# Linear-attention and feed-forward block on one core: half of the queries put with tokens on partitions, their denominators formed on VectorE

## The chip, the core and the metric

One core of one Trainium2 chip runs the whole kernel. The metric is the device time of one execution in microseconds. The kernel before took 170.02 us, the median of three runs (169.81, 170.02, 170.82).

## What is computed

The input x has 2048 tokens of 512 numbers, in bfloat16. The reference, cut to what matters:

```python
def attention(x, wqkv, wo):              # 32 heads of 16 columns
    q, k, v = split(x @ wqkv)
    phi = lambda t: jnp.where(t > 0, t + 1, jnp.exp(t)) + 1e-6
    pq, pk = phi(q), phi(k)
    kv  = einsum("bhsd,bhse->bhde", pk, v)
    z   = einsum("bhsd->bhd", pk)
    num = einsum("bhqd,bhde->bhqe", pq, kv)
    den = einsum("bhqd,bhd->bhq", pq, z)[..., None] + 1e-6
    return (num / den).reshape(B, S, D) @ wo

h  = x + attention(layernorm(x), wqkv, wo)
h2 = h + relu(layernorm(h) @ w1) @ w2    # w1 is 512 x 1792, w2 is 1792 x 512
```

There is no softmax: one 16x16 matrix kv and one vector z per head serve all tokens. The quotient num / den needs one denominator per token and head.

## The kernel before, in words

**Tiles.** The 2048 tokens are 16 tiles of 128 (t = 0 to 15) and four blocks of 512 (c = 0 to 3, four tiles each). Layer-normed tiles exist with tokens on partitions (ln_nat, which shares h_nat's memory) and transposed (lnT, columns on partitions). PSUM is one tile bk of eight banks of 128x512 float32.

**Order.** Nothing schedules the kernel: it is under a manual schedule, and a string ORDER names every operation as a word, op.index.index. A loop at the end (from L561 on) calls the functions op_... in that order. Each engine runs its own words in the order of the string, and semaphores hold back what depends on another engine. In the words of the matrix operations the last number before a slice is the PSUM bank, so the string also says which bank is reused when. All DMAs are issued by SP's queue (SyncE), in the order of the string: loads, transposes through the DMA, and the output.

**Stage 1, keys.** Per tile: bn_stats and bn_aggr (S, A, L237, L238), the reciprocal deviation on ScalarE as Ln and Exp (R, L243, L244), the normalisation (N, L262), the transpose to lnT (T on TensorE with E on ScalarE for tiles 0 to 3, X, a DMA transpose, L302, for the others), four matmuls with wk (K, L310), then phi in four instructions: Exp and Relu on ScalarE (F, U, L328, L331), min and add on VectorE (M, D, L335, L338). G (L362) accumulates layer-normed x times phi(k) over all tiles in banks 4 to 7. z (L381) sums phi(k) over the tokens.

**Stage 2, queries.** Q (L318) makes a 128x512 tile of q with *columns* on partitions and a block's 512 tokens in the free dimension; qF, qU, qM, qD (or qW, L343, which reads PSUM and does relu and add at once) turn it into phi(q), pqT. kv (L403), m (L415) and mA (L418, ScalarE, two instructions) fold kv and wo into one matrix m_sb. For a block's denominators TensorE multiplies pqT with z spread over heads (dn, L459: 16 matmuls with a free size of 8); ScalarE takes Ln (dnl, L465) and Exp of its negative, repeated 16 times per head (dnx, L472, two instructions of two tiles); the reciprocals are transposed tile by tile into rd (dt, a DMA transpose, L491; rt on TensorE with re or rv for two tiles); dm (L495, VectorE) multiplies pqT with rd into pqs, two column groups at a time. h (L505) multiplies pqs with m_sb, four matmuls per token tile, hD (L511) adds x.

**Stage 3, feed-forward.** Per tile: statistics (s, a, L239, L240), mean removed (n, L269), transpose into lnT again (x, L303, DMA). p (L521) is one of 14 column groups of the first product for a block, pA (ScalarE, L527) or pD (VectorE, L532) its relu, two groups at a time. f (L541) is the second product of a token tile, 14 matmuls in two halves of seven; fo (L549, VectorE) scales and adds h, fd (L556) stores. The products of one block lie between the attention of the next ones.

Of the kernel before, what the change touches and what calls it, by code (L numbers as in the profile page):

```python
# [9 lines left out]
ALU = mybir.AluOpType  # L10
# [20 lines left out]
Q.1.3.1 qF.1.2.2 m.0.4 m.1.5 rv.2 Q.3.1.7 qW.1.0.2 m.3.6 Q.2.3.2 dt.3 qM.1.2.2 mA.0.2 qW.1.2.2 dt.0 dt.1 m.2.5
Q.2.1.4 dn.1.0 mA.2.2 dm.0.0.2 Q.2.2.1 dm.0.2.2 dnl.1 dnx.1.2.2 h.3.6 dnx.1.0.2 h.1.5 rt.6.3 hD.3 qF.2.2.2 dt.7
s.3 re.6 h.0.0 dt.4 qU.2.2.2 hD.1 dt.5 a.3 hD.0 s.1 s.0 a.1 qM.2.2.2 a.0 Q.3.0.6 Q.2.0.3 n.3 h.2.5 n.0 dm.1.0.2
Q.3.3.1 x.3 dm.1.2.2 qF.3.0.2 hD.2 n.1 s.2 Q.3.2.0 qU.2.0.2 qF.2.0.2 h.5.2 h.6.3 a.2 qU.3.0.2 qM.2.0.2 h.4.7 n.2
qF.3.2.2 x.0 qD.2.0.2 t.2.5 qD.2.2.2 hD.4 x.1 hD.6 h.7.4 dn.2.6 hD.5 hD.7 e.2 dnl.2 qM.3.0.2 p.0.0.5 dnx.2.2.2
p.0.13.7 p.0.1.6 p.0.8.2 p.0.9.3 dnx.2.0.2 qD.3.0.2 s.4 l2.7.3 p.0.11.4 pA.0.0.2 dt.11 l2.0.3 dt.9 dt.10 r.0.4
qM.3.2.2 qW.3.2.2 s.6 dt.8 p.0.12.6 s.7 pD.0.12.2 p.0.3.1 p.0.2.0 pA.0.8.2 dn.3.2 p.0.5.7 dnl.3 p.0.4.6 a.7
dm.2.0.2 pA.0.2.2 dnx.3.0.2 dnx.3.2.2 dm.2.2.2 pD.0.4.2 h.9.0 h.8.5 p.0.6.6 p.0.7.7 dt.13 dt.12 s.5 dt.14
# [10 lines left out]
p.2.13.7 f.11.3.0.7 p.3.12.4 pD.2.12.2 f.9.6.0.7 f.9.6.7.7 f.10.7.0.7 pA.3.12.2 pA.3.0.2 f.11.3.7.7 f.10.7.7.7
f.8.2.0.7 f.12.1.0.7 f.8.2.7.7 f.14.5.0.7 f.13.4.0.7 f.15.0.0.14.3.1 f.14.5.7.7 fo.11 fo.9 fo.10 fd.10 fd.11  # L50
fo.15.3.1 fo.8 f.12.1.7.7 fd.9 f.13.4.7.7 fd.8 f.15.0.0.14.0.2 fo.14 fo.12 fd.12 fo.13 fd.15.3.1 fo.15.0.2
f.15.5.0.14.2.1 fd.13 fd.14 fd.15.0.2 fo.15.2.1 fd.15.2.1
# [4 lines left out]
def kernel(  # L57
# [10 lines left out]
    nc = tc.nc  # L68
# [41 lines left out]
    ones = const.tile([P, 1], BF16, name="ones")  # L110
# [3 lines left out]
    erep = const.tile([P, P], BF16, name="erep")  # L114
# [9 lines left out]
    z_sb = big.tile([P, KD], F32, name="z_sb")  # L124
    acts = [big.tile([P, KF, CW], BF16, name=f"at{i}") for i in range(2)]
# [15 lines left out]
    r4 = rd  # L141
# [19 lines left out]
    unit = {"k": 0, "q": NT}  # L161
# [24 lines left out]
    def op_masks():  # L186
        nc.gpsimd.memset(mask[:], 1.0)
        keep(mask3, mask3, [[-DH, P // DH], [0, DH]], 0, 1)
        keep(mask3, mask3, [[DH, P // DH], [0, DH]], DH - 1, -1)
        nc.gpsimd.memset(mask_h[:], 1.0)  # L190
        keep(mask_h[:], mask_h[:], [[0, KD], [-DH, Q4]], 0, 1)
        keep(mask_h[:], mask_h[:], [[0, KD], [DH, Q4]], DH - 1, -1)
        nc.gpsimd.memset(erep[:], 1.0)
        for q in range(KD):
            rows = erep[q * Q4 : (q + 1) * Q4, :]
            keep(rows, rows, [[1, P]], 0, -DH)
            keep(rows, rows, [[-1, P]], DH - 1, DH)
# [154 lines left out]
    op_W = lambda t, n: relu_add_of("k", t, n)  # L352
    op_qF = lambda c, j, n: exp_of("q", c * KD + j, n)
# [70 lines left out]
    def op_d4(c, b):  # L424
        at_bank["d4", c] = b
        for jb in range(KD):
            nc.tensor.matmul(
                bk[jb * Q4 : (jb + 1) * Q4, b, :], lhsT=zhd[:, jb, :], rhs=pqT[c][:, jb, :],
                start=True, stop=True,
            )  # L430

    def op_dl4(c):
        nc.scalar.activation(
            out=ld[:, c % 2, :], in_=bk[:, at_bank["d4", c], :], func=ACT.Ln, bias=eps6[:], scale=1.0
        )
# [156 lines left out]
```

## Time and profile before

| what | value |
|---|---|
| time, median of three runs | 170.02 us |
| span of the profiled execution, first to last instruction | 168.8 us |
| TensorE matmul busy | 163.1 us, 97% |
| VectorE busy | 104.4 us, 62% |
| ScalarE busy | 65.1 us, 39% |
| GpSimd busy | 4.8 us, 3% |
| share of the span on the chain that ended last, by engine | PE 85%, DVE 7%, DMA 4% |
| DMA, mean over the span | 92 GB/s |

The times listed are those of the three runs; the profiled execution is known by its span, and the median stands 1.2 us above it. PE is TensorE's matmuls, PEld its weight loads, DVE VectorE, ACT ScalarE, SPq the queue of SyncE that issues the DMAs. A matmul's duration in a row holds the depth of the array too, and consecutive matmuls overlap, so what one costs in a stream is the distance between starts: a row of the chain "76.29 3.02 PE bk L541 x14" is 14 matmuls with 512 columns in 3.02 us, 0.216 us each.

### The profile page before, as it was taken

How to read it: one execution, taken by the hardware profiler on the slowest of the kernel's cores; microseconds unless marked ns; L12 is line 12 of the kernel's file. 1: busy time of each engine (PE TensorE's matmuls, PEld its weight loads, DVE VectorE, ACT ScalarE, POOL GpSimd, SP SyncE). 2: the span in 40 equal slices, each digit the busy share in tenths (PEclk: the TensorE clock that was granted, in tenths of full speed). 3: DMA queues.
4: the chain of work that ended last, by engine and by line, in shares of the span. 5: the costliest groups of instructions: out<-in, count | busy, mean ns of one | idle time of the engine just before them, and what ended most of it. 6: DMA issues, size and time to landing. Idle time of an engine off the chain costs nothing.

```text
span 168.8 us, 2286 instructions
## 1 busy us (share of the span) xinstructions
PE 163.1 (97%) x855; PEld 78.0 (46%) x871; DVE 104.4 (62%) x205; ACT 65.1 (39%) x97; POOL 4.8 (3%) x21
## 2 busy tenths in 40 slices
PE   7989999999999999999999999999999999999993
PEld 5344344445644454444444444444444444444553
DVE  3899998997668999699819879215102432050251
ACT  3698775875879947432000003004320420400000
POOL 7400000000000000000000000000000000000000
PEclk9999999999999999999999999999999999999999
DMA  4975575689533353534130015500320000002023
GB/s 112 352 245 97 97 66 124 176 270 378 174 64 65 77 138 87 134 62 95 37 62 0 31 31 122 126 4 0 62 93 0 31 0 4 0 0 93 0 65 94
DMA packets 30491, 15.49 MB, mean 92 GB/s; under 512 B 23184, under 2 KB 29328, under 8 KB 30480
## 3 DMA queue, kind: packets, MB, share of 16 engines
q1 hardware_dynamic: 30480, 15.34, 35.5%
q8 instruction: 7, 0.11, 0.3%
q14 instruction: 4, 0.03, 0.1%
HBM read 7.86 MB, written 2.10 MB: 59 GB/s over the span
## 4 chain that ended last, share of the span: by engine, by line
PE 85%; DVE 7%; DMA 4%; issue 1%; SPq 0%
PE bk L541 29%; PE bk L521 28%; PE bk L505 8%; PE bk L318 8%; PE bk L362 6%; PE bk L310 4%; DVE st L237 3%; DMA x_nat<-in_A_x_dram 2%; DMA lnT<-h_nat 2%; DVE h_nat L262 2%; PE bk L459 1%; DVE eb L335 1%; PE bk L403 1%; PE bk L415 1%; SPq L201 0%
## 5 line engine op out<-in xcount | busy, mean ns | idle before, releaser
L541 PE MATMUL bk<-w_sb,at 128*128 128x512 bf16 (+2 forms) x247 | 50.1, 355 | 0.3
L521 PE MATMUL bk<-lnT,w_sb 128*128 128x512 bf16 x219 | 50.0, 379 | 0.3
L527 ACT ACTIVATE at<-bk 128x1024 bf16<-128x1024 f32 x14 | 14.2, 1023 | 57.4 <-PE bk L521 57.4
L541 PEld LDWEIGHTS <-at 128*128 128x128 bf16 x252 | 23.6, 98 | 25.4 <-ACT at L527 0.3
L549 DVE SCALAR_TENSOR_TENSOR gT<-bk,rstd,h_nat 128x512 bf16<-128x512 f32 (+2 forms) x18 | 12.2, 689 | 35.7 <-PE bk L541 35.6
L521 PEld LDWEIGHTS <-w_sb 128*128 128x128 bf16 x224 | 21.8, 98 | 25.8
L532 DVE TENSOR_SCALAR at<-bk 128x1024 bf16<-128x1024 f32 x14 | 17.1, 1218 | 12.8 <-PE bk L521 12.6
L328 ACT ACTIVATE eb<-bk 128x1024 bf16<-128x1024 f32 (+1 forms) x18 | 16.6, 928 | 6.6 <-PE bk L310 4.8
L310 PE MATMUL bk<-wk_sb,lnT 128*128 128x512 bf16 x63 | 15.3, 380 | 0.4 <-ACT lnT L291 0.3
L505 PE MATMUL bk<-m_sb,pqs 128*128 128x512 bf16 x63 | 15.4, 380 | 0.1
L318 PE MATMUL bk<-lnT,wq_sb 128*128 128x512 bf16 x61 | 15.1, 379 | 0.1
L362 PE MATMUL bk<-at,h_nat 128*128 128x512 bf16 x55 | 13.5, 379 | 0.1
L331 ACT ACTIVATE rb<-bk 128x1024 bf16<-128x1024 f32 (+1 forms) x14 | 12.5, 904 | 0.3 <-PE bk L310 0.3
L511 DVE TENSOR_TENSOR h_nat<-bk,x_nat 128x512 bf16<-128x512 f32 x16 | 10.5, 680 | 2.9 <-PE bk L505 2.9
L237 DVE BATCH_NORM_STATS2 st<-x_nat 128x6 f32<-128x512 bf16 x16 | 10.8, 680 | 2.4 <-DMA x_nat<-in_A_x_dram 2.4
L239 DVE BATCH_NORM_STATS2 st<-h_nat 128x6 f32<-128x512 bf16 x16 | 10.7, 683 | 0.1
L310 PEld LDWEIGHTS <-lnT 128*128 128x128 bf16 x64 | 6.0, 98 | 8.4 <-ACT lnT L291 1.0
L362 PEld LDWEIGHTS <-h_nat 128*128 128x128 bf16 x64 | 6.2, 98 | 7.4 <-issue 0.2
L505 PEld LDWEIGHTS <-pqs 128*128 128x128 bf16 x64 | 5.9, 98 | 7.9 <-DVE pqs L495 1.8
L318 PEld LDWEIGHTS <-wq_sb 128*128 128x128 bf16 x64 | 5.9, 98 | 6.4
L472 ACT ACTIVATE wk_sb<-ld 128x1024 bf16<-128x1024 f32 x8 | 8.1, 1050 | 0.1
L335 DVE TENSOR_SCALAR eb<-eb 128x1024 bf16<-128x1024 bf16 (+1 forms) x18 | 6.8, 383 | 0.9 <-ACT eb L328 0.9
(63 smaller groups left out, 93.5 us busy)
## 6 DMA issues: line engine op xcount, KB each, us to landing
out_dram<-gT SPq DMA_DIRECT2D x15, 128.0 KB, 1.9
w_sb<-in_B_w_dram SPq DMA_DIRECT2D x2, 896.0 KB, 9.8
x_nat<-in_A_x_dram SPq DMA_DIRECT2D x2, 512.0 KB, 6.3
w_sb<-in_B_w_dram SPq DMA_DIRECT2D x2, 512.0 KB, 9.5
x_nat<-in_A_x_dram SPq DMA_DIRECT2D x3, 256.0 KB, 4.6
w_sb<-in_B_w_dram SPq DMA_DIRECT2D x2, 384.0 KB, 3.5
wk_sb<-in_A_wqkv_dram SPq DMA_DIRECT2D x2, 256.0 KB, 4.3
wq_sb<-in_A_wqkv_dram SPq DMA_DIRECT2D x2, 256.0 KB, 4.9
```

What stands on the lines that cost most here:

```text
L237: op_S = lambda t: nc.vector.bn_stats(out=st[:, t, :], in_=x_nat[:, t, :])
L310: nc.tensor.matmul(bk[:, b, :], lhsT=lnT[c][:, kd, j * P : (j + 1) * P], rhs=wk_sb[:, kd, :], start=(kd == 0), stop=(kd == KD - 1),)
L318: nc.tensor.matmul(bk[:, b, :], lhsT=wq_sb[:, kd, j * P : (j + 1) * P], rhs=lnT[c][:, kd, :], start=(kd == 0), stop=(kd == KD - 1),)
L328: nc.scalar.activation(out=buf(eb, kind, i, n), in_=bank(at_bank[kind, i], n), func=ACT.Exp)
L331: nc.scalar.activation(out=buf(rb, kind, i, n), in_=bank(at_bank[kind, i], n), func=ACT.Relu)
L362: nc.tensor.matmul(bk[:, KD + kd, :], lhsT=ln_nat[:, t, kd * P : (kd + 1) * P], rhs=pk(t)[:, 0, :], start=(t == 0), stop=(t == NT - 1),)
L505: nc.tensor.matmul(bk[:, b, :], lhsT=pqs[:, (c * KD + jb) % NQ, j * P : (j + 1) * P], rhs=m_sb[:, jb, :], start=(jb == 0), stop=(jb == KD ...
L521: nc.tensor.matmul(bk[:, b, cols], lhsT=w1_sb[:, kd, f * P : (f + 1) * P], rhs=lnT[c][:, kd, cols], start=(kd == 0), stop=(kd == KD - 1),)
L527: nc.scalar.activation(out=acts[c % 2][:, f : f + n, :], in_=bank(at_bank["p", c, f], n), func=ACT.Relu)
L532: nc.vector.tensor_scalar(out=acts[c % 2][:, f : f + n, :], in0=bank(at_bank["p", c, f], n), scalar1=0.0, scalar2=None, op0=ALU.max,)
L541: nc.tensor.matmul(bk[:, b, 0 : w * P], lhsT=acts[c % 2][:, f, j * P : (j + 1) * P], rhs=w2_sb[:, f, k * P : (k + w) * P], start=(f == 0), ...
L549: nc.vector.scalar_tensor_tensor(out=o_t[:, t % NO, cols], in0=bk[:, at_bank["f", t, k], 0 : w * P], scalar=rstd2[:, t : t + 1], in1=h_nat ...
```

## The change

Blocks 0 and 1 keep their way. For blocks 2 and 3 (tiles 8 to 15):

- Y takes Q's place: four matmuls per *token tile* with lnT as the stationary side and wq as the moving one, so that phi(q) comes out with tokens on partitions. The words yF, yU, yM, yD do what qF, qU, qM, qD do, two tiles at a time; the words qW are gone.
- The denominators are not made by TensorE any more (dn.2, dn.3, with their dnl, dnx, dt and dm, are gone). z is first spread over 128 identical rows: zd (VectorE) makes four diagonal matrices, zr (TensorE) multiplies them with ones, four matmuls with 128 columns, and zC (ScalarE) copies the result to zrep. Then per two tiles: dT (VectorE) multiplies phi(q) with zrep into float32 products, dR (VectorE) sums each 16 of them, dl and dx (ScalarE) take Ln and the repeated Exp, dy (VectorE) multiplies phi(q) in place.
- The quotient is then transposed tile by tile to pqs by a DMA transpose (ty). h and all that follows stay.
- Of the relus of the first product, pA has 12 instead of 14 instructions and pD 16 instead of 14. re now does both copies of rd from PSUM (rv is gone), and qU and qD take the place of two qW of block 1.
- The whole ORDER is written anew. The first two Y stand between the last Q and h of block 0. The attention of blocks 2 and 3 now lies between the second products of block 0 and those of block 1. Loads of wv, wq, wo and w2 are put in among the first transposes.
- The constant erep, which nothing read, is gone; ones grows to 128x128.

```diff
-Q.1.3.1 qF.1.2.2 m.0.4 m.1.5 rv.2 Q.3.1.7 qW.1.0.2 m.3.6 Q.2.3.2 dt.3 qM.1.2.2 mA.0.2 qW.1.2.2 dt.0 dt.1 m.2.5
+dnx.0.0.2 dnx.0.2.2 l1.2.2 l1.0.2 dt.1 dt.3 dt.0 qF.1.0.2 qU.1.0.2 rt.2.7 Q.1.3.6 Y.14.4 kx m.1.1 m.0.0 qF.1.2.2
...
+    def op_Y(t, b):
+        c, j = divmod(t, CT)
+        at_bank["y", t] = b
+        for kd in range(KD):
+            nc.tensor.matmul(
+                bk[:, b, :], lhsT=lnT[c][:, kd, j * P : (j + 1) * P], rhs=wq_sb[:, kd, :],
+                start=(kd == 0), stop=(kd == KD - 1),
+            )
...
+    def op_zd():
+        nc.vector.tensor_tensor(
+            out=zdg[:], in0=ident.rearrange("p (o n) -> p o n", o=1).broadcast_to([P, KD, P]), in1=z_on(P),
+            op=ALU.mult,
+        )
+
+    def op_zr(b):
+        at_bank["zr"] = b
         for jb in range(KD):
             nc.tensor.matmul(
...
+                bk[:, b, jb * P : (jb + 1) * P], lhsT=ones[:], rhs=zdg[:, jb, :], start=True, stop=True
+            )
+
+    def op_zC():
+        nc.scalar.activation(out=zrep[:], in_=bank(at_bank["zr"]), func=ACT.Copy)
+
+    def toks(t, n):
+        return pqT[t // CT][:, t % CT : t % CT + n, :]
+
+    def op_dT(t, n):
+        nc.vector.tensor_tensor(
+            out=prod[:, 0:n, :], in0=toks(t, n), in1=zrep.broadcast_to([P, n, D]), op=ALU.mult
+        )
+
+    def op_dR(t, n):
+        nc.vector.tensor_reduce(
+            out=den[:, t * H : (t + n) * H], in_=prod[:, 0:n, :].rearrange("p t (h r) -> p (t h) r", r=DH),
+            axis=mybir.AxisListType.X, op=ALU.add,
+        )
+
+    def op_dl(t, n):
+        cols = den[:, t * H : (t + n) * H]
+        nc.scalar.activation(out=cols, in_=cols, func=ACT.Ln, bias=eps6[:], scale=1.0)
+
+    def op_dx(t, n):
+        src = den[:, t * H : (t + n) * H].rearrange("p (h o) -> p h o", o=1)
...
+            out=rn[:, t % CT : t % CT + n, :].rearrange("p t (h r) -> p (t h) r", r=DH),
+            in_=src.broadcast_to([P, n * H, DH]), func=ACT.Exp, scale=-1.0,
+        )
+
+    def op_dy(t, n):
+        nc.vector.tensor_tensor(out=toks(t, n), in0=toks(t, n), in1=rn[:, t % CT : t % CT + n, :], op=ALU.mult)
+
+    def pqs_of(t):
+        c, j = divmod(t, CT)
+        i = c * KD % NQ
+        return pqs[:, i : i + KD, j * P : (j + 1) * P]
+
+    def op_ty(t):
+        nc.sync.dma_start_transpose(out=pqs_of(t), in_=toks(t, 1)[:, 0, :])
```

**ScalarE, from the reciprocals of block 0 to the folded matrix.** Before, L465 is dnl, L472 dnx, L328 qF, L418 mA:

```order
L465 ACTIVATE ld<-bk,eps_74 128x128
L472 ACTIVATE wk_sb<-ld 128x1024
L328 ACTIVATE eb<-bk 128x1024
L472 ACTIVATE wk_sb<-ld 128x1024
L328 ACTIVATE eb<-bk 128x1024
L418 ACTIVATE m_sb<-bk 128x1024 x2
L465 ACTIVATE ld<-bk,eps_74 128x128
```

Now, with the line numbers of the changed kernel (L504 dnl, L511 dnx, L334 qF, L337 qU, L522 re, L429 mA):

```order
L504 ACTIVATE ld<-bk,eps_74 128x128
L511 ACTIVATE wk_sb<-ld 128x1024 x2
L334 ACTIVATE eb<-bk 128x1024
L337 ACTIVATE rb<-bk 128x1024
L334 ACTIVATE eb<-bk 128x1024
L337 ACTIVATE rb<-bk 128x1024
L522 ACTIVATE rd<-bk 128x4x128
L429 ACTIVATE m_sb<-bk 128x1024 x2
L504 ACTIVATE ld<-bk,eps_74 128x128
```

The two dnx stand together, and two qU and one re have come between them and the two mA; before, relu and add of block 1 were VectorE's (L343), and so was the copy into rd.

**VectorE, in the first product of block 0.** Before, L338 and L343 end the phi of the last queries, L239 is s, L532 pD, L495 dm of block 2, L511 hD:

```order
L335 TENSOR_SCALAR eb<-eb 128x1024
L343 SCALAR_TENSOR_TENSOR pqT_88<-bk,eb 128x1024
L239 BN_STATS st_101<-h_nat 128x6 x2
L532 TENSOR_SCALAR at_94<-bk 128x1024
L240 BN_AGGR mv_102<-st_101 128x2
L495 TENSOR_TENSOR pqs<-pqT_87,rd 128x1024 x2
L532 TENSOR_SCALAR at_94<-bk 128x1024
L239 BN_STATS st_101<-h_nat 128x6
L511 TENSOR_TENSOR h_nat<-bk,x_nat 128x512
L239 BN_STATS st_101<-h_nat 128x6
```

Now (L344 yD, L550 hD, L236 s, L455 dT, L571 pD, L266 n, L460 dR):

```order
L344 TENSOR_TENSOR pqT_86<-rb,eb 128x1024
L236 BN_STATS st_104<-h_nat 128x6
L455 TENSOR_TENSOR prod<-pqT_86,zrep 128x1024
L571 TENSOR_SCALAR at_97<-bk 128x1024 x2
L266 TENSOR_SCALAR hn<-h_nat,mv_105 128x512
L237 BN_AGGR mv_105<-st_104 128x2
L266 TENSOR_SCALAR hn<-h_nat,mv_105 128x512
L236 BN_STATS st_104<-h_nat 128x6
L571 TENSOR_SCALAR at_97<-bk 128x1024
L237 BN_AGGR mv_105<-st_104 128x2
L266 TENSOR_SCALAR hn<-h_nat,mv_105 128x512
L460 TENSOR_REDUCE den<-prod 128x64
```

The multiplication by z and the reductions stand in the same queue as the relus of the first product and the means that the transposes of block 1 wait for.

**SyncE's queue, in the first 25 us.** Before, L201 and L204 are loads, L302 the transposes of stage 1:

```order
L201 DMA x_nat<-in_A_x_dram 128x2048 x2
L204 DMA wq_sb<-in_A_wqkv_dram 128x2x512
L302 DMA_TRANSPOSE lnT_82<-h_nat 128x4x128 x4
L302 DMA_TRANSPOSE lnT_83<-h_nat 128x4x128 x2
L302 DMA_TRANSPOSE lnT_84<-h_nat 128x4x128 x2
L302 DMA_TRANSPOSE lnT_83<-h_nat 128x4x128 x2
L204 DMA wq_sb<-in_A_wqkv_dram 128x2x512
L302 DMA_TRANSPOSE lnT_84<-h_nat 128x4x128 x2
```

Now (L198, L201 loads, L299 transposes):

```order
L201 DMA wv_sb<-in_A_wqkv_dram 128x2x512
L198 DMA x_nat<-in_A_x_dram 128x2048
L201 DMA w_sb<-in_B_w_dram 128x3x512
L299 DMA_TRANSPOSE lnT_81<-h_nat 128x4x128 x2
L201 DMA wq_sb<-in_A_wqkv_dram 128x2x512
L299 DMA_TRANSPOSE lnT_81<-h_nat 128x4x128 x2
L201 DMA w_sb<-in_B_w_dram 128x4x512
L299 DMA_TRANSPOSE lnT_82<-h_nat 128x4x128
L201 DMA wq_sb<-in_A_wqkv_dram 128x2x512
L299 DMA_TRANSPOSE lnT_82<-h_nat 128x4x128
L299 DMA_TRANSPOSE lnT_83<-h_nat 128x4x128 x2
L201 DMA wo_sb<-in_A_wo_dram 128x2x512
```

Loads of wv, wq, w2 and wo now stand ahead of and between the transposes, where before a single load of wq stood ahead of ten transposes.

More of the change, by code (lines that the diff above doesn't have):

```diff
@@ L34 @@
[L34 to L38, printed above, removed]
@@ L49 @@
[L49 to L52, printed above, removed]
+table lx.0.1 lx.1.1 lx.2.2 lk.0.2 masks lx.4.2 const S.0 lk.2.2 lx.6.2 A.0 warmf.4.3 S.1 lx.8.4 R.0.1 lv.2.2 A.1
@@ L109 @@
     eps6 = const.tile([P, 1], F32, name="eps6")
-    ones = const.tile([P, 1], BF16, name="ones")
+    ones = const.tile([P, P], BF16, name="ones")
     ident = const.tile([P, P], BF16, name="ident")
@@ L192, in op_masks @@
         keep(mask_h[:], mask_h[:], [[0, KD], [DH, Q4]], DH - 1, -1)
[L193 to L197, printed above, removed]
     def op_lx(t, n):
@@ L381, in op_z @@
             nc.tensor.matmul(
-                bk[:, b, jb : jb + 1], lhsT=part[:, jb * P : (jb + 1) * P], rhs=ones[:],
+                bk[:, b, jb : jb + 1], lhsT=part[:, jb * P : (jb + 1) * P], rhs=ones[:, 0:1],
                 start=(i == 0), stop=(i == len(parts) - 1),
@@ L440, in op_rp @@
-    def op_rp(c, jb, b):
-        at_bank["rp", c, jb] = b
-        rows = slice(jb * Q4, (jb + 1) * Q4)
-        nc.tensor.matmul(
-            bk[:, b, :], lhsT=erep[rows, :], rhs=r4[rows, c, :], start=True, stop=True
-        )
-    def op_rm(c, jb, n):
-        i = (c * KD + jb) % NQ
-        nc.vector.tensor_tensor(
-            out=pqs[:, i : i + n, :], in0=bank(at_bank["rp", c, jb], n), in1=pqT[c][:, jb : jb + n, :],
-            op=ALU.mult,
-        )
+            out=rn[:, t % CT : t % CT + n, :].rearrange("p t (h r) -> p (t h) r", r=DH),
@@ L454, in op_dn, with op_rE @@
+    def op_rE(t):
+        nc.scalar.activation(out=pqs_of(t), in_=at_bank["ry", t], func=ACT.Copy)
     def op_dn(c, b):
```

79 lines of the change are left out of this document (44 added, 35 removed).

## The prediction

> **What bounds the kernel now.** I read the page first, then the chain of work that ended last, then the timeline around each wait of the chain, and the groups by line and shape for durations.
>
> ```profile
> PE 163.1 (97%) x855; PEld 78.0 (46%) x871; DVE 104.4 (62%) x205; ACT 65.1 (39%) x97; POOL 4.8 (3%) x21
> ...
> PEclk9999999999999999999999999999999999999999
> DMA  4975575689533353534130015500320000002023
> ```
>
> TensorE is busy 97% of the span at full granted clock. The chain says the same in order of time (start, length, what):
>
> ```profile
> 41.53 0.38 PE bk L459 x16
> ...
> 42.79 0.89 PE bk L403 x16
> ...
> 50.35 1.97 PE bk L505 x8
> ...
> 61.40 0.38 PE bk L459 x16
> ...
> 69.57 0.38 PE bk L459 x16
> ...
> 71.70 2.00 PE bk L505 x8
> ...
> 76.29 3.02 PE bk L541 x14
> ...
> 166.18 0.35 DVE gT L549
> ```
>
> From 21.1 to 166.2 us every piece of the chain is TensorE, but for slivers of 0.05 called issue. 14 matmuls of 512 columns take 3.02 us, so 0.216 each: that is the price of TensorE's work here, and there is little beside it. The two pieces of eight L505 show what waiting is left: eight cost 1.73, and they took 1.97 and 2.00, so 0.24 and 0.27 us were lost to pqs that came late. One more wait is in the start:
>
> ```profile
> 10.85 14.66 SPq L302 DMA_TRANSPOSE lnT<-h_nat  x10
> ...
> 19.94 1.03 PE L362 MATMUL bk<-at,h_nat 128*128 128x512 bf16 x4
> ...
> 21.09 0.55 PEld L310 LDWEIGHTS <-lnT 128*128 128x128 bf16 x4 [0.63 <-DMA lnT<-h_nat]
> 21.10 1.04 PE L310 MATMUL bk<-wk_sb,lnT 128*128 128x512 bf16 x4
> ```
>
> Four matmuls from 19.94 would end their slots at 20.80; the next begins at 21.10, when a transpose has landed: 0.30 lost. So from about 10 us on the whole kernel gives away some 0.8 us, and the change can win only by taking work from TensorE or by these 0.8. It can lose wherever the new order makes TensorE wait.
>
> **TensorE's work.** Y has as many matmuls of 512 columns as the Q it replaces: 32 for 32, nothing. dn.2 and dn.3 go: the pieces at 61.40 and 69.57, 0.76 us. zr is four matmuls of 128 columns; 16 of that width (L403) took 0.89, so 0.056 each and 0.22 together. The counts of transposes, of warming matmuls and of halves of f are the same. Net **-0.54 us**, and it counts in full since nothing but TensorE is on the chain there.
>
> **The folded matrix comes later.** ScalarE between the denominators of block 0 and m_sb:
>
> ```profile
> 28.27 1.02 ACT L331 ACTIVATE rb<-bk 128x1024 bf16<-128x1024 f32 x1
> ...
> 29.18 1.03 ACT L328 ACTIVATE eb<-bk 128x1024 bf16<-128x1024 f32 x1
> ...
> 30.08 1.04 ACT L331 ACTIVATE rb<-bk 128x1024 bf16<-128x1024 f32 x1
> ...
> 41.37 0.54 PE L459 MATMUL bk<-zhd,pqT 128*128 128x8 bf16 x16
> ...
> 41.95 0.37 ACT L465 ACTIVATE ld<-bk,eps 128x128 f32<-128x128 f32 x1
> ...
> 49.91 2.00 ACT L472 ACTIVATE wk_sb<-ld 128x1024 bf16<-128x1024 f32 x2
> ...
> 52.72 0.59 ACT L483 ACTIVATE rd<-bk 128x512 bf16<-128x512 bf16 x1
> ```
>
> Back to back, an Exp or Relu of 128x1024 starts 0.91 after the one before it (28.27, 29.18, 30.08). dnl starts at 41.95; nothing ahead of it on ScalarE or TensorE is changed in amount, so I keep that. Then, start to start: dnl 0.40, two dnx 1.94, four qF and qU 3.64, re 0.55, first mA 0.91, and the second mA takes 1.02 to its end: 41.95 + 8.46 = 50.4. The new qU are what makes it late; qW on VectorE kept ScalarE free. TensorE, from dn.0 at 41.37: dn 0.38, kv 0.89, two Q 1.73, rt 0.22, Q 0.86, three Y 2.59, four m 0.86, dn.1 0.38, zr 0.22, sum 8.13: h begins at 49.5. Its first two matmuls need only the first half of m_sb and pqs; the third, due at 49.93, waits for 50.4. **+0.5 us.** pqs is ready by then: the first dnx ends at 43.4, three DMA transposes at most 1.47 us apart (ten in 14.66, above) and 2.5 from the last issue to its landing give 48.8, and two dm of 0.69 make 50.2.
>
> ```profile
> rd<-wk_sb SPq DMA_TRANSPOSE x14, 2.5
> lnT<-h_nat SPq DMA_TRANSPOSE x12, 2.5
> ```
>
> Block 1 follows from there: dnl, dnx, yF, yU, dnx end near 54.5, the last dt lands at 57.1, the second dm ends near 58.5, and h.5, due at 58.0, needs it in its third matmul: **+0.1**. Some 0.1 more lies in kv and dn.1, which meet their inputs to within 0.1. Against these stand the two losses of before at pqs, **-0.51**, for the words that met them there are gone or are the ones just counted. Sum of this stage: +0.2 of waits over before.
>
> **VectorE's new denominators.** What they cost is in no row; the nearest:
>
> ```profile
> L532 DVE TENSOR_SCALAR at<-bk 128x1024 bf16<-128x1024 f32 x14 | 17.1, 1218 | 12.8 <-PE bk L521 12.6 <-remote 0.2
> ...
> L549 DVE SCALAR_TENSOR_TENSOR gT<-bk,rstd,h_nat 128x512 bf16<-128x512 f32 x15 | 11.1, 748 | 27.0 <-PE bk L541 26.9
> ...
> L239 DVE BATCH_NORM_STATS2 st<-h_nat 128x6 f32<-128x512 bf16 x16 | 10.7, 683 | 0.1
> L511 DVE TENSOR_TENSOR h_nat<-bk,x_nat 128x512 bf16<-128x512 f32 x16 | 10.5, 680 | 2.9 <-PE bk L505 2.9
> ...
> L369 DVE TENSOR_TENSOR at<-at,at 128x1024 f32<-128x1024 f32 x5 | 6.1, 1223 | 0.1
> ...
> L335 DVE TENSOR_SCALAR eb<-eb 128x1024 bf16<-128x1024 bf16 x14 | 5.7, 414 | 0.9 <-ACT eb L328 0.9
> L269 DVE TENSOR_SCALAR hn<-h_nat,mv 128x512 bf16<-128x512 bf16 x16 | 5.3, 342 | 0.1
> L495 DVE TENSOR_TENSOR pqs<-pqT,rd 128x1024 bf16<-128x1024 bf16 x8 | 5.2, 687 | 2.8 <-DMA rd<-wk_sb 2.6 <-issue 0.2
> ...
> L240 DVE BATCH_NORM_AGGREGATE mv<-st 128x2 f32<-128x6 f32 x16 | 2.6, 170 | 0.1
> ```
>
> dT reads two bf16 and writes float32: between 0.69 (L495, all bf16) and 1.22 (L369, all float32); I take 1.22, as it writes what L369 writes. dR reads 1024 float32 and writes 64: at least 0.41 (L335, the cheapest pass over 1024), at most 2.4 (twice L369, if a pass costs each of its short sums something); 1.22 again, and L239, a reducing pass over 512 in 0.68, points there. The Trainium skill (VectorE: DVE Perf Modes, "The perf-mode tier table") says that tensor_reduce has only the slowest mode, one element per cycle whatever the type, and its cycle table would make that 1.13 us for 1024 elements, an estimate of that page; with it the sum below would be shorter by 0.3 us.
>
> ```profile
> 60.99 2.48 DVE L511 TENSOR_TENSOR h_nat<-bk,x_nat 128x512 bf16<-128x512 f32 x4
> ```
>
> ```profile
> 60.00:80.00 20.00, 19.89 (x121) 9.31 (x123) 17.89 (x31) 9.60 (x13) 0.00 (x0) 1.00 0.46 106
> 80.00:100.00 20.00, 19.89 (x92) 9.11 (x93) 14.42 (x32) 0.50 (x2) 0.00 (x0) 1.00 0.13 27
> ```
>
> In these windows (PE, PEld, DVE, ACT, POOL busy) VectorE had 2.1 and 5.6 us free and ScalarE 10.4 and 19.5, so there is room, but the queue is in order. From the first dm of block 1 (57.1) to the second dy, which releases ty for h.15, VectorE has 2 dm, 4 hD, 5 s with 5 a and 5 n, 4 yM, 4 yD, 4 dT, 3 dR, 4 pD, 2 fo, 2 dy: 44 instructions, 29.6 us by row means (yD as dm), some 27 if each starts 0.06 before the end of the last, as four L511 in 2.48 instead of 2.72 do. With 2.5 for the transpose pqs is there between 86.6 and 89.3. TensorE from h.5 (58.0) to h.15 has 4 h, t, 14 p, 7 halves of f, 3 p, 2 h: 30.7 us, 88.7. Slack between -0.6 and 2.1, middle 0.8. I put **0** in the sum and keep +0.6 for the range. dl, dx and zC are covered by ScalarE's free time; were that gone, an ACT pair would cost 1.4 per two tiles. The banks of the first product (pD behind dT) come free with 0.5 to spare by the same addition.
>
> **The start.** 1664 KB of loads (384 + 512 of w2, two of 256 of wq, 256 of wo) now lie ahead of or between the first ten transposes, where 256 KB lay.
>
> ```profile
> w_sb<-in_B_w_dram SPq DMA_DIRECT2D x2, 384.0 KB, 3.5
> ```
>
> ```profile
> 17.65 3.40 DMA lnT<-h_nat
> ```
>
> ```profile
> PEld L310 <- DMA lnT<-h_nat: 1.0, 2, 0.6
> ```
>
> One transpose took 3.40 from issue to landing, and that made the 0.30 of before, the longer of two waits. Now the transposes of tiles 8 and 9 each follow a load (512 and 256 KB) directly, and the matmuls that read them stand at nearly the same places of TensorE's order as before. Two transposes at 3.4 instead of 2.5 give up to +1.8; if all fits, -0.3 is regained. The nearest row is the old wait: I take **+0.2**. The end is as before: the same last half rows, then fo and one store.
>
> **Sum.** -0.54 + 0.2 + 0 + 0.2 = -0.14: a span of 168.8 - 0.1 = 168.7 us, and with the 1.2 us by which the median stands above the span, **169.9 us**. Its own range, from the bounds above (start -0.3 to +1.8, VectorE 0 to +0.6, waits ±0.3): 168.9 to 171.3.
>
> **Rivals.** *The new order closes the gaps.* Then -0.54, -0.8 of old waits and none new, at most 0.3 more from the start: 168.4. For it: each wait that I found is 0.5 or less, within the error of such additions. Against: m_sb's 0.5 comes from ten instructions in a queue whose distances are measured.
>
> *The reductions bound the feed-forward stage (slower).* dR of tiles 10, 8 and 14 stand ahead of the dy that h.15 needs. With a slack of 0.8 it decides from 1.5 us per dR on; at the bound of 2.4 it costs 3 x 1.18 - 0.8 = 2.7: 172.6. For it: 64 short sums per instruction have no row here. Against: L239 and L369. The same page of the Trainium skill, "Rules for kernel authors", calls tensor_reduce the slowest VectorE operation and advises against it on a hot path; no run shows it yet.
>
> *Loads delay the first transposes (slower).* From 10 to 25 us the DMA row shows five to seven tenths with transposes almost alone. 1664 KB more at the page's best 378 GB/s are 4.5 us of 15, three tenths. It decides from a landing time of about 3 us on, and at 3.4 or more for the transposes of tiles 9 and 13 it costs 1.3 beside the +0.2: 171.2.
>
> ```profile
> GB/s 112 352 245 97 97 66 124 176 270 378 174 64 65 77 138 87 134 62 95 37 62 0 31 31 122 126 4 0 62 93 0 31 0 4 0 0 93 0 65 94
> ```
>
> **How the numbers follow.** A measurement of this kernel can tell about 1%, 1.7 us, from no change. Chances: the forecast 0.58, closed gaps 0.14, reductions 0.11, loads 0.17. Faster by over 1% means under 168.3: more than half of the closed gaps' 0.14 and a little of the forecast, 0.10. Slower by over 1%, above 171.7: most of the reductions' 0.11 and a third of the loads' 0.17, 0.14. Within 1%: 0.76. The range reaches down to the closed gaps and up past the loads: 168.4 to 171.6.
>
> **What would show it.** Right: L459 with 32 matmuls and 1.1 us busy; a wait of near 0.5 us before the third matmul of the first h, ended by m_sb on ScalarE; TENSOR_REDUCE near 1.2 us; waits on TensorE from 60 us on below 0.5 in all. Wrong: TENSOR_REDUCE above 1.5 with TensorE waiting for pqs or for a bank that pD frees; PEld waits on DMA lnT<-h_nat above 1.3 us (now 1.0); or a span under 167.5, which my waits at m_sb do not allow.

## The result, and the profile after

The changed kernel took 172.13 us (median of four runs, 171.58 to 172.34); the kernel before, on the same chip, 170.38 us (169.81 to 170.82). The ratio is 1.0106, 95% interval 1.007 to 1.0142: 1.75 us slower, where 169.9 us was forecast. The profiled execution took 171.92 us with a span of 170.2.

The page after, busy time of each engine, the granted clock and the DMA engines' share in 40 slices:

```profile
PE 163.8 (96%) x843; PEld 77.2 (45%) x843; DVE 115.7 (68%) x215; ACT 66.9 (39%) x102; POOL 2.3 (1%) x12
...
PE   7999969999999999999999999999999999999993
...
PEclk9999999999999999999999999999999999999999
DMA  4997899993040530014313350055400000000322
```

TensorE still has the end, at full clock. Its first slice under 9 after the warming is the sixth, 21.3 to 25.5 us, and there the DMA engines are full where they had been five to seven tenths. Windows of the span after (length, then busy time of PE, PEld, DVE, ACT, POOL, then clock, DMA share, GB/s) put the loss into one of them:

```profile
20.00:40.00 20.00, 18.31 (x85) 7.97 (x84) 17.63 (x32) 11.37 (x16) 0.00 (x0) 1.00 1.07 249
60.00:80.00 20.00, 20.00 (x97) 9.12 (x96) 19.89 (x36) 8.25 (x12) 0.00 (x0) 1.00 0.17 34
80.00:100.00 20.00, 20.00 (x95) 9.09 (x93) 17.61 (x25) 4.98 (x7) 0.00 (x0) 1.00 0.34 67
100.00:160.00 60.00, 60.00 (x287) 27.85 (x286) 25.83 (x41) 9.47 (x14) 0.00 (x0) 1.00 0.16 38
```

From 60 us on TensorE never waits, though VectorE is busy 19.89 of 20 us where its new denominators begin. All that was lost, was lost early. The waits after (engine, line, releaser, total, times, longest):

```profile
PEld L307 <- DMA lnT<-h_nat: 3.7, 5, 1.7
```

This row stood at 1.0 before, and 1.3 was the mark that the prediction set for being wrong. L307 is K, the keys; L299 is X, its DMA transpose. The timeline of SyncE's queue, and below it TensorE's:

```profile
17.59 1.19 SPq L299 DMA_TRANSPOSE lnT<-h_nat  x1
18.83 0.58 SPq L201 DMA_DIRECT2D wq_sb<-in_A_wqkv_dram  x1
19.51 3.81 SPq L299 DMA_TRANSPOSE lnT<-h_nat  x3
```

```profile
19.34 1.89 PE L373 MATMUL bk<-at,h_nat 128*128 128x512 bf16 x8
21.70 1.04 PE L307 MATMUL bk<-wk_sb,lnT 128*128 128x512 bf16 x4 [0.46 <-DMA lnT<-h_nat]
23.96 1.04 PE L307 MATMUL bk<-wk_sb,lnT 128*128 128x512 bf16 x4 [1.23 <-DMA lnT<-h_nat]
```

Eight matmuls from 19.34 fill their slots until 21.07, at 0.216 each; the keys of tile 8 begin at 21.70: 0.63 lost. Those four end their slots at 22.56, and the keys of tile 9 begin at 23.96: 1.40 lost. Together 2.0 us, where the same place lost 0.30 before. The transpose of tile 8, issued at 17.59 behind a load of 512 KB, landed just ahead of 21.70, 4.1 us later; that of tile 9, issued behind the load at 18.83, is the longest piece of the chain there:

```profile
19.51 4.41 DMA lnT<-h_nat
```

### The profile page after: what moved, and what is told of

Same layout as the page of the kernel before. It is cut to its first block, busy times and chain, and to the rows that moved or that the text cites. A ratio compares the mean times of both kernels' runs of the same rounds, so it can differ in the third digit from the quotient of the medians.

```text
span 170.2 us, 2241 instructions
## 1 busy us (share of the span) xinstructions
PE 163.8 (96%) x843; PEld 77.2 (45%) x843; DVE 115.7 (68%) x215; ACT 66.9 (39%) x102; POOL 2.3 (1%) x12
## 4 chain that ended last, share of the span: by engine, by line
PE 79%; DVE 7%; ACT 6%; DMA 4%; issue 1%
PE bk L580 28%; PE bk L560 28%; PE bk L544 8%; PE bk L373 5%; PE bk L307 4%; DVE st L234 3%; DMA lnT<-h_nat 3%; PE bk L315 3%; PE bk L324 3%; DMA x_nat<-in_A_x_dram 2%; ACT eb L334 2%; ACT rb L337 2%; DVE h_nat L259 1%; ACT m_sb L429 1%; DVE at L344 1%
## 5 line engine op out<-in xcount | busy, mean ns | idle before, releaser
L560 PE MATMUL bk<-lnT,w_sb 128*128 128x512 bf16 x224 | 50.0, 379 | 0.0
L560 PEld LDWEIGHTS <-w_sb 128*128 128x128 bf16 x224 | 21.9, 98 | 26.2
L566 ACT ACTIVATE at<-bk 128x1024 bf16<-128x1024 f32 x12 | 12.3, 1021 | 52.5 <-PE bk L560 52.5
L588 DVE SCALAR_TENSOR_TENSOR gT<-bk,rstd,h_nat 128x512 bf16<-128x512 f32 (+2 forms) x18 | 12.1, 688 | 24.6 <-PE bk L580 20.3
L571 DVE TENSOR_SCALAR at<-bk 128x1024 bf16<-128x1024 f32 x16 | 19.2, 1219 | 13.5 <-PE bk L560 13.5
L334 ACT ACTIVATE eb<-bk 128x1024 bf16<-128x1024 f32 (+1 forms) x18 | 16.5, 928 | 5.5 <-PE bk L307 5.5
L307 PE MATMUL bk<-wk_sb,lnT 128*128 128x512 bf16 x64 | 15.7, 380 | 1.9 <-DMA lnT<-h_nat 1.7
L337 ACT ACTIVATE rb<-bk 128x1024 bf16<-128x1024 f32 (+1 forms) x17 | 15.7, 924 | 3.2 <-PE bk L315 3.1
L544 PE MATMUL bk<-m_sb,pqs 128*128 128x512 bf16 x64 | 15.3, 379 | 0.1
L550 DVE TENSOR_TENSOR h_nat<-bk,x_nat 128x512 bf16<-128x512 f32 x16 | 10.8, 679 | 1.8 <-PE bk L544 1.8
L236 DVE BATCH_NORM_STATS2 st<-h_nat 128x6 f32<-128x512 bf16 x16 | 10.9, 688 | 0.2
L307 PEld LDWEIGHTS <-lnT 128*128 128x128 bf16 x64 | 5.8, 98 | 10.0 <-DMA lnT<-h_nat 3.7
L544 PEld LDWEIGHTS <-pqs 128*128 128x128 bf16 x64 | 6.1, 98 | 7.4 <-DVE pqs L534 0.5
L240 ACT ACTIVATE rstd<-mv,eps 128x2 f32<-128x2 f32 (+2 forms) x14 | 4.2, 299 | 10.3 <-DVE mv L237 5.3
L315 PE MATMUL bk<-lnT,wq_sb 128*128 128x512 bf16 x32 | 8.0, 379 | 0.0
L324 PE MATMUL bk<-wq_sb,lnT 128*128 128x512 bf16 x32 | 7.6, 379 | 0.0
```

Of the source, the lines that this page charges most:

```text
L307: nc.tensor.matmul(bk[:, b, :], lhsT=lnT[c][:, kd, j * P : (j + 1) * P], rhs=wk_sb[:, kd, :], start=(kd == 0), stop=(kd == KD - 1),)
L315: nc.tensor.matmul(bk[:, b, :], lhsT=wq_sb[:, kd, j * P : (j + 1) * P], rhs=lnT[c][:, kd, :], start=(kd == 0), stop=(kd == KD - 1),)
L324: nc.tensor.matmul(bk[:, b, :], lhsT=lnT[c][:, kd, j * P : (j + 1) * P], rhs=wq_sb[:, kd, :], start=(kd == 0), stop=(kd == KD - 1),)
L334: nc.scalar.activation(out=buf(eb, kind, i, n), in_=bank(at_bank[kind, i], n), func=ACT.Exp)
L337: nc.scalar.activation(out=buf(rb, kind, i, n), in_=bank(at_bank[kind, i], n), func=ACT.Relu)
L544: nc.tensor.matmul(bk[:, b, :], lhsT=pqs[:, (c * KD + jb) % NQ, j * P : (j + 1) * P], rhs=m_sb[:, jb, :], start=(jb == 0), stop=(jb == KD ...
```

## The experiments

The theory after the result: the loads put among the first transposes delay them, and nothing else of the change costs anything. The rivals: the new order of keys and evictions makes the waits by itself; VectorE's denominators or the later folded matrix cost, and the start hides it. All ratios are to the kernel before on the same chip; medians of before were 169.9 to 170.0 us there.

### Loads moved off the transposes (a_loads_back), and only five of them (d_few)

```diff
 a_loads_back, in ORDER of the change:
-lv.2.2 l2.0.3 lq.2.2 l2.10.4 lq.0.2 lo.2.2 l2.3.4 lv.0.2 l2.7.3 lo.0.2 (among X.4 to X.15), l1.2.2 l1.0.2
+lq.0.2 behind lx.12.4; lq.2.2 behind X.13; lv, lo and l1 behind X.14; l2 behind x.3
 d_few, in ORDER of the change:
-lv.2.2 l2.0.3 l2.10.4 lq.0.2 lo.2.2 (ahead of and between X.4 to X.10)
+lq.0.2 behind lx.12.4; l2.10.4 lo.2.2 lv.2.2 l2.0.3 behind X.14
```

> The changed kernel with its loads moved off the first transposes, nothing else: one half of wq ahead of the ten transposes (256 KB, as in the kernel before), the other after the eighth, wv, wo and w1 after the twelfth, w2 after the first transposes of stage 3. Theory (loads in the same queue delay the transposes of tiles 8 and 9, and TensorE loses 2.0 us there): both transposes land about 2.5 us after issue, TensorE's waits at L307 fall from 2.0 to 0.3 us or less, span 168.2 to 168.5, ratio to the kernel before 0.995 to 0.999. Rival (VectorE's new order issues the two transposes too late, loads or not): the wait stays above 1 us, span above 169.5, ratio 1.005 or more.

> The change with only the loads that stand ahead of the transposes of tiles 8 and 9 moved out of their way (one load of queries' weights and the later loads stay among the transposes). If only loads right ahead of a transpose that TensorE waits for count, this is as good as all loads moved back: 1.003 to 1.006. If every load among the transposes costs its share: 1.007 to 1.010.

Measured: a_loads_back 170.54 us, ratio 1.0041 (1.0025 to 1.0056), between the two expectations; d_few 170.50 us, 1.0042 (1.0027 to 1.0058), as the first of its two said. So the loads account for 0.65 of 1.06%, 1.1 us, and five of the twelve, those right ahead of the transposes of tiles 8 and 9 among them, for all of that. Some 0.8 us must have another cause. The waits, the timeline of TensorE and one piece of the chain of a_loads_back show where it lies:

```profile
PEld L306 <- DMA lnT<-h_nat: 2.9, 4, 1.1
```

```profile
20.26 1.03 PE L306 MATMUL bk<-wk_sb,lnT 128*128 128x512 bf16 x4
21.86 1.04 PE L306 MATMUL bk<-wk_sb,lnT 128*128 128x512 bf16 x4 [0.56 <-DMA lnT<-h_nat]
...
23.59 1.03 PE L306 MATMUL bk<-wk_sb,lnT 128*128 128x512 bf16 x4
25.27 1.04 PE L306 MATMUL bk<-wk_sb,lnT 128*128 128x512 bf16 x4 [0.65 <-DMA lnT<-h_nat]
```

```profile
21.00 4.23 DMA lnT<-h_nat
```

The keys of tile 8 (20.26) wait no more. Those of tile 9 begin 0.74 us behind the end of the slots ahead of them (21.12), where the change lost 1.40, and those of tile 13 begin 0.82 behind (24.45). So the wait fell to 1.56 and not to the 0.3 that I expected. The transpose of tile 9, the sixth, landed after 3.5 us and that of tile 13, the eighth, after 4.23, though no load was issued from 5.12 until 22.26.

### The kernel before, with the new places of the loads (b_before_loads)

```diff
 ORDER of before:
-lq.2.2 lv.0.2 lv.2.2 l1.0.2 l2.10.4 lo.0.2 lo.2.2 l2.3.4 l1.2.2 l2.7.3 l2.0.3 (at their later places)
+l2.0.3 behind lq.0.2, lq.2.2 behind X.4, l2.10.4 behind X.6, lv.0.2 behind X.9, lo.2.2 behind X.13,
+l2.3.4 lv.2.2 l2.7.3 lo.0.2 behind X.10, l1.2.2 l1.0.2 behind X.14
```

> The kernel before with the changed kernel's order of loads among the first twelve transposes, nothing else (w2's 384 KB ahead of the first, 256 KB of wq after the second, 512 KB of w2 after the fourth, 256 KB after the fifth, 256 KB of wo after the eighth, the rest after the tenth). Theory of the loads: the fifth and sixth transposes land 4 us after issue, TensorE waits 1.5 to 2.0 us more there, ratio 1.009 to 1.012. Rival (VectorE's new order): the old order keeps its waits, ratio 1.000 to 1.003.

Measured: 173.74 us, 1.0221 (1.0195 to 1.0247), twice as much. The direction is that of the theory; the size is explained only in part. The trace is of the longest of the six executions (174.48 us). The timeline of TensorE and a window:

```profile
15.62 1.03 PE L360 MATMUL bk<-at,h_nat 128*128 128x512 bf16 x4
17.24 1.04 PE L308 MATMUL bk<-wk_sb,lnT 128*128 128x512 bf16 x4 [0.59 <-DMA lnT<-h_nat]
...
18.98 1.03 PE L308 MATMUL bk<-wk_sb,lnT 128*128 128x512 bf16 x4
22.12 1.04 PE L308 MATMUL bk<-wk_sb,lnT 128*128 128x512 bf16 x4 [2.11 <-DMA lnT<-h_nat]
...
24.36 1.92 PE L308 MATMUL bk<-wk_sb,lnT 128*128 128x512 bf16 x4
```

```profile
23.00:27.00 4.00, 4.00 (x12) 1.50 (x11) 1.35 (x4) 0.69 (x1) 0.00 (x0) 0.57 0.75 131
```

TensorE lost 0.76 us ahead of 17.24, and stood still from 19.84 (18.98 and four slots) to 22.12, 2.28 us. Then the granted clock fell to 0.57 over 23 to 27 us: four matmuls took 1.92 instead of 1.04, some 1.7 us lost again. But that fall belongs to this one execution. Its mean granted clock is 0.990, that of the other five is 1.000, and their spans are still 171.2 to 172.2 us, where the kernel before has 168.1. So in those five the loads cost 3 to 4 us without any fall of the clock, more than the 2.7 that the two waits add here (0.76 and 2.28 less the old 0.30); where the rest went is open: no trace shows it. The 1.40 us of the change had no such sequel. The Trainium skill (TensorE: Matmul & The Clock Gate, "Why this matters for your kernels") asks for no idle gap over about 3 us if the clock is to stay; here, in one execution of six, a gap of 2.28 us was followed by the fall.

### The reductions doubled (c_reduce_twice)

```diff
 ORDER of the change, each of the four:
-dR.10.2
+dR.10.2 dR.10.2
```

> The changed kernel with each of the four reductions done twice in a row (the second writes the same numbers again): 4.8 us more on VectorE, 3.6 of it ahead of the multiplication that the first product of tile 15 with m_sb waits for. Theory (the reductions are covered, but with about 1.6 us to spare by the trace, where that tile's transpose landed at 89.06 for a need at 90.66): TensorE waits about 2 us there and in what follows, ratio 1.020 to 1.026 to the kernel before. Rival (ample cover, VectorE idle time absorbs it): the time of the changed kernel, 1.010 to 1.013. Rival (no cover, every us on VectorE counts): 4.8 us more, 1.037 or above.

Measured: 176.42 us, 1.0375 (1.0349 to 1.0401). The groups of VectorE, first of the change, then of this kernel:

```profile
L455 DVE TENSOR_TENSOR prod<-pqT,zrep 128x1024 f32<-128x1024 bf16 x4 | 4.9, 1219 | 0.1
L460 DVE TENSOR_REDUCE den<-prod 128x64 f32<-128x1024 f32 x4 | 4.8, 1211 | 0.0
```

```profile
L460 DVE TENSOR_REDUCE den<-prod 128x64 f32<-128x1024 f32 x8 | 9.7, 1216 | 0.1
```

TensorE in this kernel (L544 is h, L560 p, L588 fo, L550 hD):

```profile
87.56 1.03 PE L544 MATMUL bk<-m_sb,pqs 128*128 128x512 bf16 x4
89.30 1.02 PE L560 MATMUL bk<-lnT,w_sb 128*128 128x512 bf16 x4 [0.71 <-DVE gT L588]
90.16 1.03 PE L544 MATMUL bk<-m_sb,pqs 128*128 128x512 bf16 x4
92.36 1.04 PE L544 MATMUL bk<-m_sb,pqs 128*128 128x512 bf16 x4 [1.18 <-DMA pqs<-pqT]
93.23 1.03 PE L560 MATMUL bk<-lnT,w_sb 128*128 128x512 bf16 x4
95.35 1.02 PE L560 MATMUL bk<-lnT,w_sb 128*128 128x512 bf16 x4 [1.09 <-DVE h_nat L550]
96.73 2.96 PE L560 MATMUL bk<-lnT,w_sb 128*128 128x512 bf16 x12 [0.36 <-DVE gT L588]
```

4.9 us more on VectorE cost 4.6 us by the ratios (1.0375 less 1.0106) and 3.7 by the profiled spans (173.9 less 170.2). By the slots of the timeline TensorE lost 0.88 and 1.34 us up to the product of tile 15 (92.36), behind three of the four added reductions, so of their 3.6 us 1.4 were covered, near the 1.6 that I expected. What I left out comes behind it: 1.26 and 0.52 us of waiting for banks that hD and fo free, as VectorE's queue is late by then. Of all 4.9 us 4.0 were lost, 0.9 covered: enough for the change, where TensorE waits for nothing, and little more.

### One eviction back on VectorE (e_back_qw)

```diff
 ORDER of a_loads_back:
-qU.1.2.2
-qD.1.2.2
+qW.1.2.2 (at qD's place)
```

> The kernel with the loads moved back, and in it the second half of block 1's relu and add done in one VectorE instruction from PSUM, as in the kernel before (one ScalarE instruction of 1.0 us less ahead of m_sb, VectorE 1.2 instead of 0.7 us). Theory (ScalarE's queue makes m_sb late by about half a us): that wait falls by 0.3 to 0.5 us against the kernel with the loads moved back, span 167.8 to 168.2. Rival (pqs on VectorE ends just as late, so nothing is won): same span as the kernel with the loads moved back within 0.2 us.

Measured: 170.81 us, 1.0055 (1.0037 to 1.0073), no better than the 1.0041 it started from. The wait only moved, by TensorE's timeline of this kernel:

```profile
47.39 1.89 PE L323 MATMUL bk<-wq_sb,lnT 128*128 128x512 bf16 x8
49.52 0.59 PE L425 MATMUL bk<-wo_sb,kvbd 128*128 128x512 bf16 x2 [0.24 <-DVE pqT L348]
```

Eight slots from 47.39 end at 49.12; the folding product m.2 begins at 49.52, as its bank is freed by the slower qW. So the rival's outcome came (169.0 us of span, 168.9 without this step): the earlier folded matrix is worth nothing here.

### The old start with the new rest (f_start_before), and the reverse (g_start_after)

```diff
 f_start_before, ORDER of the change up to zh:
-table lx.0.1 ... gA.0.2 gA.2.2 z.1.3.14 ... zc zh
+(ORDER of before) const lx.0.1 ... z.3.3.14 ... zc gA.0.2 gA.2.2 zh
 and from Q.1.0.1 dn.0.4 on as the change, with lo.2.2 l2.3.4 l1.2.2 ahead of dt.1 and l2.0.3 l2.7.3 behind x.3
 g_start_after: ORDER of the change up to zh, then ORDER of before from Q.1.0.2 on, l1.0.2 behind dnl.0
```

> The change with the start of the kernel before put back: every word up to the copy of the Gram matrix, loads among the transposes included, stands as before, and all that follows (spread attention, denominators by VectorE, projections with tokens on partitions) as in the change. If all the loss lies in the first 30 us (2.0 us of TensorE's waiting there instead of 0.3), TensorE loses 1.7 us less than in the change: span 168.3 to 168.6, ratio to before 0.995 to 0.999, and TensorE waits less than 0.4 us for the transposes. If the part behind it costs something of its own that the start's delay now hides (the folded matrix, VectorE's denominators), the ratio is 1.002 or more and the waits stand behind 45 us.

> The other half: the kernel before with the change's first part (loads, transposes, keys and Gram products in its order), and the denominators and the attention as before. If the loss lies in the start, it is here in full: TensorE waits about 2 us at the keys of tiles 8 and 9, span 170.4 to 170.9, ratio 1.009 to 1.013. If the spread attention carries the loss: 1.000 to 1.005.

Measured: f_start_before 169.78 us, 0.9996 (0.9983 to 1.0009), span 168.3; g_start_after 172.88 us, 1.0182 (1.0141 to 1.0223). The first answers the question, though 0.9996 lies just above the range that I gave for it. With the old start, all of the loss is gone, and the rest of the change, which is all that its name speaks of, is neither gain nor loss within 0.2%. The waits of f_start_before:

```profile
PEld L543 <- DVE pqs L533: 1.0, 3, 0.5
PEld L306 <- DMA lnT<-h_nat: 1.0, 2, 0.6
```

The lnT row is that of before again. The second kernel lost what the change lost in its start, and more. Its TensorE:

```profile
6.38 0.58 PE L279 MATMUL bk<-ident,h_nat 128*128 128x128 bf16 x4 [0.92 <-POOL ident masks.py:199]
...
7.65 2.74 PE L308 MATMUL bk<-wk_sb,lnT 128*128 128x512 bf16 x6
```

The old constants include erep, eight selections on GpSimd, which the new order puts ahead of the identity: TensorE's first transposes wait 0.92 us, and the six key matmuls behind them take 2.74 us, where four at full speed take 1.04. That is my experiment's own cost: its first denominators' matmul begins at 44.56 us where the change's begins at 43.39. So its size says little, and the verdict rests on f_start_before.

### Other work ahead of a late transpose (h_gram_first)

```diff
 ORDER of a_loads_back:
-K.13.3 F.12.2 za.2 G.6
+G.6 K.13.3 F.12.2 za.2
```

> The kernel with all loads moved back, and the four Gram products of tile 6 (0.86 us, ready 3 us earlier) put ahead of the keys of tile 13, which waited 0.65 us for their late transpose. If what was left of the loss is the order of the new start against transposes that land late without any load near, these 0.65 us go: ratio 0.998 to 1.001 where 1.0041 was measured. If the wait only moves to the next keys or to the eviction of these: 1.003 to 1.005.

Measured: 170.74 us, 1.006 (1.0041 to 1.008): no gain. The timeline of TensorE:

```profile
25.47 1.04 PE L306 MATMUL bk<-wk_sb,lnT 128*128 128x512 bf16 x4
...
38.93 1.89 PE L372 MATMUL bk<-at,h_nat 128*128 128x512 bf16 x8 [0.34 <-DVE at L348]
42.26 0.56 PE L497 MATMUL bk<-zhd,pqT 128*128 128x8 bf16 x16 [0.17 <-DVE zhd L400]
```

The keys of tile 13 wait for nothing now, as intended. But they begin no earlier (25.27 in a_loads_back), so VectorE's chain behind the keys is as late as before, and TensorE, having spent its spare work, waits for that chain at 38.9 and 42.3 instead. So a late transpose delays not TensorE alone but the evictions of its keys, and filling TensorE's gap did not pay here. That the rest of the loss comes from an order that wants tiles 9 and 13 before they have landed fits this, but is argued, not shown.

### Two steps past both kernels (i_copies_first, j_two_behind)

```diff
 i_copies_first, ORDER of f_start_before:
-lo.2.2 l2.3.4 l1.2.2 dt.1 dt.3 dt.0
+dt.1 dt.3 dt.0 lo.2.2 l1.2.2 l2.3.4
 j_two_behind:
+lo.2.2 dt.1 dt.3 dt.0 l1.2.2 l2.3.4
```

> The kernel with the old start, and its three late loads (second half of the output projection's weights, and two of the feed-forward weights) issued behind the first block's three DMA transposes of reciprocals instead of ahead of them. Those transposes landed 3.0, 2.4 and 2.5 us after their issue with the DMA engines full until 45 us, and the first attention matmul waited 0.6 us in all behind them. If a load ahead of a DMA transpose is what delays it, these 0.4 to 0.6 us go: ratio to before 0.996 to 0.998, faster than both kernels. If the wait moves to the folded matrix or to the loads themselves: 0.999 to 1.001.

> As the kernel with the old start, with only the two late feed-forward loads (512 and 384 KB) issued behind the first block's three transposes of reciprocals; the output projection's second half goes out early again, since as a late load it kept the folding products waiting 1.6 us (issued 46.78, landed 49.72). In that run the three transposes each landed 2.4 us after issue and the wait for the scaled queries was 0.06 us instead of 0.6. Here both waits should be gone: ratio to before 0.996 to 0.998. If the folded matrix, whose copy ends last then, takes the wait over: 0.999 to 1.001.

(The two feed-forward loads are 896 and 512 KB by the profile's DMA part, not 512 and 384 as I wrote there.) Measured: i_copies_first 171.46 us, 1.009 (1.0076 to 1.0103); j_two_behind 169.72 us, 0.9986 (0.9976 to 0.9997). The first moved one load too many. Its wait for it:

```profile
PEld L425 <- DMA wo_sb<-in_A_wo_dram: 1.9, 1, 1.9
```

Half of wo, issued at 46.78 behind the transposes, came late for the folding products. With that load early again, the first attention products of j_two_behind begin 0.21 us behind the end of zr's four slots of 0.054, in f_start_before 0.39:

```profile
49.27 0.38 PE L443 MATMUL bk<-zdg,ones 128*128 128x128 bf16 x4
49.70 3.62 PE L543 MATMUL bk<-m_sb,pqs 128*128 128x512 bf16 x15
```

```profile
49.30 0.38 PE L443 MATMUL bk<-zdg,ones 128*128 128x128 bf16 x4
49.91 3.36 PE L543 MATMUL bk<-m_sb,pqs 128*128 128x512 bf16 x14 [0.22 <-DVE pqs L533]
```

(The first fence is j_two_behind, the second f_start_before.) It beats both kernels: the change by 1.2%, the kernel before by 0.14%, less than expected.

## Why the prediction was wrong

**The step that failed** is the term of the start, "I take **+0.2**", with its ground "The nearest row is the old wait". It measured +1.7 by the timeline (2.0 less the old 0.3), and 1.9 us (1.0106 to 0.9996) by putting the old start back. The rest of the sum, -0.34, came out at -0.07 (0.9996 of 169.92 us; -0.29 to +0.15 by the interval), a far smaller error. Three things were wrong in that one term.

*The landing time.* I bounded two transposes by the one 3.4 that the chain showed, +1.8 at most, and then took the value nearest to no change. They landed after 4.1 and 4.4 us, each right behind a load. The trace of before held a longer landing than 3.4, off the chain and with no load near. Its DMA part from 21.2 to 22 us, where the eighth transpose is issued:

```profile
lnT<-h_nat SPq DMA_TRANSPOSE x1, 4.1
```

Two at 4.1 instead of 2.5 would have given +3.2. Nor is all of the 4.4 the loads': the sixth transpose takes 3.4 before and 3.5 in a_loads_back, so there they add 0.9, and to the fifth, which landed after 2.4 in both, some 1.6. The 1664 KB of the prediction also leave out the 256 KB of wv that stand ahead of the first transpose. "Loads delay the first transposes", the third rival, had the mechanism and the sign, at 0.17. Its own measure came out: it "decides from a landing time of about 3 us on". Its price, 1.3, was near the 1.1 us that the loads cost by a_loads_back.

*The order of the keys.* That "the matmuls that read them stand at nearly the same places of TensorE's order" does not hold. The old ORDER has four matmuls of the Gram sum (G.4) between the keys of tiles 9 and 8, twelve (G.5 to G.7) behind them, and four (G.9) between the keys of tiles 12 and 13; the new one has K.8 and K.9 side by side, and K.12 and K.13. Nor did I ask what VectorE behind it does. With the loads away, 0.8 us stayed. The old order had the same late transposes, 3.4 and 4.1 us, and lost 0.30 to them. The rival of closed gaps fell with both.

*The distance from the bound to the choice.* Range and bound were on the page: +1.8 would have given 171.5 us, still 0.6 short. The unknown was larger than every other term, and I let a row from a queue without loads choose it.

**The terms that held.** TensorE's work: the denominators' matmuls are 32 with 1.1 us busy and zr four matmuls, as taken.

```profile
L498 PE MATMUL bk<-zhd,pqT 128*128 128x8 bf16 x32 | 1.1, 167 | 0.0
...
L444 PE MATMUL bk<-zdg,ones 128*128 128x128 bf16 x4 | 0.4, 217 | 0.0
```

That this is worth 0.54 us in time is not shown: f_start_before gained 0.04% (0.17% at best, 0.09% lost at worst), j_two_behind 0.14%. By the traces the time from the first matmul of dn.0 to the start of the last fo fell from 124.81 us before to 124.15 in the change and 124.49 in f_start_before, but the trace of before is of a long execution, as said below. VectorE's denominators at 0: dT 1.219 and dR 1.211 us against 1.22 taken, and no wait from 60 us on; the rival of the reductions fell. (The 44 instructions of VectorE add up to 30.8 us by the rows, not to the 29.6 of the prediction; in the trace they took 27.5, from 59.04 to 86.57, near its lower value of 27.) The prediction's estimate from the Trainium skill (VectorE: DVE Perf Modes, "The perf-mode tier table", and that page's cycle table), 1.13 us, is 7% short of the trace. The folded matrix: the third attention matmul waited 0.26 us for m_sb where 0.5 was taken, so the middle came out near 0 instead of +0.2.

**The span and the time.** I added 1.2 us from span to time, one execution's span against the median of three others. In runs that list both, the time is 1.7 us above the span (171.92 and 170.2, 170.02 and 168.3). By the executions of before in the later runs, the median span is 168.1 to 168.3, so the 168.8 that the sum began from was a long one. The two errors cancel: 168.8 and 1.2 make 170.0, the median time of before.

**What stays open.** Why the sixth and the eighth transpose of the first block are late with no load near: after 3.4 and 4.1 us in the kernel before, 3.4 and 3.7 in f_start_before, 3.5 and 4.2 in a_loads_back, where their neighbours land after 2.4 to 2.8. In the DMA part of before, from 18.5 to 25.5 us:

```profile
q8 instruction: 1, 0.02, 0.8%
q14 instruction: 1, 0.01, 0.5%
```

Two packets of kind "instruction", of 16 and 8 KB, lie among the transposes, and the same ones among those of a_loads_back. Two shorter windows of before, 18.7 to 19.9 and 19.9 to 21.5 us, show more:

```profile
q1 hardware_dynamic: 536, 0.13, 56.3%
q14 instruction: 1, 0.01, 2.8%
...
q1 hardware_dynamic: 552, 0.13, 42.9%
```

One transpose is 544 packets (as in the window of the fifth, 17.4 to 18.6). Of the sixth, 536 moved in the first window together with the instruction packet, and eight came only in the second, with the 544 of the seventh. So the sixth was late by its last eight packets. That the instruction packet held them up is an argument from place and time; no kernel here moved it. How much of the remaining 0.8 us is due to these late landings and how much to the order that meets them sooner was not separated.

## What to carry to other kernels

A change named for its arithmetic may lie elsewhere: read the rewritten order from its first word, and price each transfer that is moved ahead of a transfer that somebody waits for, at the longest landing in the whole trace (here 4.1 us), not at the median nor at the longest on the chain. When such a term has the widest bounds of the sum, take its middle or worse, and let the range reach past the bound. To find which part of a rewritten order costs, join the old first part to the new rest at a place where few things are in flight: that one kernel settled here what the others had only narrowed.

## What the runs showed of the hardware

In one of six executions of b_before_loads a stretch of 2.28 us without matmuls was followed by a granted clock of 0.57 over 4 us; stretches of 1.40 us in the change and of 1.34 in c_reduce_twice left it at 1.00. DMA transposes of 128x512 mostly landed 2.4 to 2.8 us after issue with no load near, but two of them after 3.4 and 4.1 (before), and the change's landed after 3.1 to 4.4 right behind a load of 256 or 512 KB in the same queue. A sum over 16 neighbours of 128x1024 float32 (TENSOR_REDUCE) takes 1.21 us, as much as the 1.22 of a multiplication that writes float32: these short sums carried no surcharge.
